# mLSTM cell and cosine-gated MLP on one core: the head's decay sums moved from VectorE subtractions to TensorE products and a GpSimd mask

## The chip, the cores and the metric

The kernel runs on 1 core of one Trainium2 chip. The metric is device time in microseconds of one execution; the figure compared is the median of several runs. A core has TensorE (PE in the profile; its weight loads are PEld), VectorE (DVE), ScalarE (ACT), GpSimd (POOL) and SyncE (SP), which here only issues DMAs.

## The reference

The program is an mLSTM cell with stabilised exponential gates, followed by an MLP whose gate is h cos h. Shapes: 4 batches, 8 heads, 768 steps, 40 dimensions a head; the MLP has 3072 rows, 320 to 2048 to 320.

```python
def _attn_ref(q, k, v, i_gate, f_gate, o_gate):
    for t in range(S):
        m_new = np.maximum(f_gate[:, :, t] + m, i_gate[:, :, t])
        f_stab = np.exp(f_gate[:, :, t] + m - m_new)
        i_stab = np.exp(i_gate[:, :, t] - m_new)
        m = m_new
        C = f_stab * C + i_stab * np.einsum('bhd,bhe->bhde', vt, kt)
        n = f_stab * n + i_stab * kt
        h_tilde = np.einsum('bhde,bhe->bhd', C, qt)
        denom = np.maximum(np.abs(np.einsum('bhd,bhd->bh', n, qt)), 1.0)
        y[:, :, t] = sigmoid(o_gate[:, :, t]) * h_tilde / denom

def _moe_ref(x, w_in, w_out):
    h = x @ w_in
    g = h * np.cos(h)
    return g @ w_out
```

## The kernel before, in words

The 768 steps are cut into six chunks of 128 (`NC`), and each chunk has four cells, one for each batch (`B`), with its eight heads: 24 cells, numbered n = 4 x chunk + batch. Inside a cell the recurrence is written as a masked matrix product. With F the running sum of f_gate, a = i_gate - F and M the running maximum of a, the weight of step s in the output of step t is exp(a[s] - M[t]) for s up to t and zero above. The tile `E` of a cell (128 source steps by 8 heads by 128 target steps) holds these weights; `decay` makes the exponential, `weigh` multiplies E by the scores k q (a product in PSUM), `values` multiplies by v, `normalize` divides by the denominator and applies the output gate into the tile y (one buffer), and `seam` turns y into the layout of the MLP and makes the cell's increment of the state from `kw` (`weigh_k`, on GpSimd). `seam_out` copies the turned y into xT and xL; `state` copies or adds the increment.

The order of all instructions is written by hand (`tc.manual_schedule()`): each engine runs its part of the list in that order, and waits in it hold up everything behind them on that engine. `first_cells` is the head: the four cells of chunk 0, the gates of all later chunks, and the first weights of the MLP. Then `first_period` starts the MLP of chunk 0 (`Up`: products L749 with w_in_sb, L743 with w_in_l; `near` on ScalarE, L757, is the first reader of their sums) along with cell 4, and the later functions pair MLP blocks with cells to the end.

In the head, the gates of chunk 0 are scanned first (`gates_first`). M and its exact split into three bfloat16 parts (`maxima_in_parts`) go to TensorE: for each cell `maxima_in` puts into two PSUM banks a wall of 1e30 above the diagonal (`wall_in`, L442) and on top the maxima spread over all source steps (`spread`, L449). `less_sums` (L467, VectorE) subtracts a from the banks into E, and `decay` takes exp(-E), so the wall becomes zero.

The gates of chunks 1 to 5 are in five tiles of 32 rows by 640: `gates_sums` (a scan on VectorE), `gates_less_sums` (GpSimd), `gates_maxima` (the second, long scan, and the write of M to DRAM, `M_d`), `gates_shifts`, `gates_carry` (five activations on ScalarE, and the write `G_d`), `gates_exp` (five activations on ScalarE: exp(a - the chunk's last maximum)), `gates_turn` (TensorE transposes of a and of that exponential, L325) and `gates_turn_out` (L328, one copy into `tab`, which the later cells read). `load_M` reads a cell's maxima back from M_d into E, spread over 128 rows (L436); `load_G_of` does the like with G_d.

The weights come as doubles and are turned into float32 in pieces: `take_apart` (ScalarE, L175 and L177), `bound` (VectorE, L181 and L182), `join` (VectorE, L191), `round_up` (GpSimd, L196). `weights_in(0)` issues the loads of three such pieces on SyncE: pieces 0 and 1 of w_in (L163, four DMAs each) and the piece w_in_l (L217). `warm` (L1096) issues products of zeros whose result nobody reads. PSUM is handed out in four rotating banks in the pool `ps_o`, two in `ps_a` and two in `ps_u`; a bank is given again when its last reader is done. `odd_constants` is four GpSimd memsets.

Of the kernel before, what the change touches and what calls it, by code (L numbers as in the profile page):

```python
# [11 lines left out]
FP = mybir.dt.float32  # L12
I32 = mybir.dt.int32
U32 = mybir.dt.uint32
BF = mybir.dt.bfloat16
AF = mybir.ActivationFunctionType
OP = mybir.AluOpType
# [12 lines left out]
def kernel(  # L30
# [56 lines left out]
    yo = small[:, 384:384 + DM]  # L87
    M0_parts = small[:, 704:768].bitcast(BF)
    of_parts = small[:, 768:784].bitcast(BF)
    nc.vector.memset(nil, 0.0)  # L90
    ident = const.tile([128, 128], FP, name="ident")
    make_identity(nc, ident)
# [6 lines left out]
    firsts = blocks[:, 32:36]  # L99
    nc.vector.memset(M0_parts, 0.0)  # L100
    nc.vector.memset(of_parts, 0.0)

    nc.gpsimd.memset(wall, 0.0)
    nc.gpsimd.affine_select(out=wall, in_=wall, compare_op=OP.is_ge, fill=1.0e30, base=0,
# [134 lines left out]
    m0 = gates.tile([BH, R], FP, name="m0")  # L239
    nM1 = gates.tile([BH, R], FP, name="nM1")  # L240
    dd = gates.tile([BH, R - 1, BH], FP, name="dd")

    def gates_constants():
        nc.gpsimd.memset(keep, 1.0)
# [22 lines left out]
    def maxima_in_parts():  # L267
# [7 lines left out]
        nc.vector.tensor_copy(out=M0_parts[2 * BH:3 * BH], in_=rest)  # L275
        nc.scalar.copy(out=M0_parts[BH:2 * BH], in_=mid)

    def gates_first_out():
        pg = ps_o.tile([128, 2, BH], FP, name="pg", tag="o")
        for j, src in enumerate((a0, e0)):  # L280
            nc.tensor.transpose(pg[:, j], src, ident[0:BH, 0:BH])
        nc.vector.tensor_copy(out=tab[:, 0, 0:2], in_=pg)
# [1 line left out]
    last = slice(C - 1, C)  # L284
    flat = [t.rearrange("r c s -> r (c s)") for t in (F1, M1, a1, keep, shift)]

    eW, eG = shift, keep

    def gates_sums():
        nc.vector.tensor_tensor_scan(out=flat[0], data0=flat[3], data1=flat[0], initial=0.0, op0=OP.mult, op1=OP.add)  # L290

    def gates_less_sums():
        nc.gpsimd.tensor_tensor(out=a1, in0=a1, in1=F1, op=OP.subtract)
        nc.gpsimd.tensor_copy(out=shift[:, 0, 0:1], in_=F0[:, last])
        nc.gpsimd.tensor_copy(out=shift[:, 1:R, 0:1], in_=F1[:, 0:R - 1, last])
# [15 lines left out]
        for j in range(2):  # L311
            nc.gpsimd.dma_start(out=dst[j], in_=eG[j:BH:2])

    def gates_exp():
        for c in range(R):
            nc.scalar.activation(out=eW[:, c], in_=a1[:, c], func=AF.Exp, bias=nM1[:, c:c + 1])

    def gates_diagonal():

        nc.vector.tensor_tensor(out=dd, in0=ident[0:BH, 0:BH].unsqueeze(1).to_broadcast([BH, R - 1, BH]),  # L320
                                in1=eG[:, 0:R - 1, last].to_broadcast([BH, R - 1, BH]), op=OP.mult)

    def gates_turn(pg, j):
        for c in range(R):
            nc.tensor.transpose(pg[:, c, j], (a1, eW)[j][:, c], ident[0:BH, 0:BH])  # L325

    def gates_turn_out(pg):
        nc.scalar.copy(out=tab[:, 1:NC, 0:2], in_=pg)  # L328

    def gates_spread():  # L330
        pd = ps_o.tile([128, R - 1, BH], FP, name="pd", tag="o")
# [38 lines left out]
    def sigmoid(c, bs=slice(0, B)):  # L370
        if c == 0:
            o = sig[c][:, bs]
            nc.scalar.activation(out=o, in_=o, func=AF.Sigmoid)
            return
        place_gates(c, AF.Sigmoid)
# [92 lines left out]

    def decay(n, heads=range(H)):
        c, b = divmod(n, B)  # L470
        if n < B:
            nc.scalar.activation(out=Es[n], in_=Es[n], func=AF.Exp, scale=-1.0)
            return
        for h in heads:
            g = b * H + h
            nc.scalar.activation(out=Es[n][:, h], in_=Es[n][:, h], func=AF.Exp, scale=-1.0, bias=tab[:, c, 0, g:g + 1])  # L476
# [91 lines left out]
    def values(n):  # L568
        pool, tag = psum(n)
        E = Es[n]  # L570
        if n < B:
            ph = pool.tile([128, H, D1], FP, name="ph", tag=tag)
            for j in range(2):
                for p in range(HP):
                    h = 2 * p + j
                    nc.tensor.matmul(ph[:, h], E[:, h], vs(n)[:, h, 0:D1], start=True, stop=True)  # L576
            heads_of[n] = ph
            return
        vt = pool.tile([128, 4, C], FP, name="vt", tag=tag)
        state = st[n % B]  # L580

        for i in range(3):
            if i < 2:
                for a in range(HP):
                    h = 2 * a + i
                    nc.tensor.matmul(vt[32 * a:32 * a + 32, i], vs(n)[:, h, 0:32], E[:, h], start=True, stop=False)  # L586
            else:
                for a in range(HP):
                    nc.tensor.matmul(vt[32 * a:32 * a + 32, i], vr2[n // 2 % 2][:, n % 2, a, 1:3].rearrange("q g d o -> q (g d o)"),
                                     E[:, 2 * a + 1], start=True, stop=False)  # L590
                for a in range(HP):
                    nc.tensor.matmul(vt[32 * a:32 * a + 16, i], vr2[n // 2 % 2][:, n % 2, a, 0].rearrange("q d o -> q (d o)"),
                                     E[:, 2 * a], start=False, stop=False)
            for a in range(HP):
                nc.tensor.matmul(vt[32 * a:32 * a + 32, i], state[:, ts(HP * i + a, 32)], Gs[n][:, a], start=False, stop=True)  # L595
        heads_of[n] = vt
# [501 lines left out]
    def maxima_in(n):  # L1098
        for i in range(2):
            wall_in(n, i, psum_o())  # L1100
        for i in range(2):
            spread(n, i)

    def less_sums(n):
        for i in range(2):
            decay_exponents_half(n, i)

    def first_cells():
        gates_in()
        nc.scalar.copy(out=ident_b, in_=ident)  # L1110
        for i in range(3):
            r = ts(i, BH)
            nc.scalar.copy(out=of_parts[r], in_=ident[r, r])
        load(0, "qk")
        gates_constants()
        ones_of_values()
        later_gates_in()
        load(0, "v")
        load(1, "qk")
        load_o(0)  # L1120
        load(1, "v")
        load(2, "qk")
        warm(9)
        wall_in(0, 0, pmu)
        gates_first()
        for n in range(B):
            load_E(n)
        load(2, "v")
        load(3, "qkv")
        maxima_in_parts()  # L1130
        gates_first_out()
        wall_in(0, 1, psum_o())
        for i in range(2):
            spread(0, i)
        for i in range(2):
            decay_exponents_half(0, i)
        turn(0)
        turn_out(0, False)
        decay(0)
        maxima_in(1)  # L1140
        less_sums(1)
        weigh_k(0)
        blocks_constants()
        weigh_k(1)
        state_constants()
        scores(0)
        turn(1)
        decay(1)
        turn_out(1, False)
        weigh(0)  # L1150
        sigmoid_next()
        sigmoid(0)
        exp_next()
        gates_sums()
        gates_less_sums()
        values(0)
        pieces.extend(weights_in(0))
        scores(1)
        weigh(1)
        maxima_in(2)  # L1160
        less_sums(2)
        decay(2)
        values(1)
        normalize(0)
        normalize(1)
        maxima_in(3)
        less_sums(3)
        turn(2)
        turn_out(2, False)
        weigh_k(2)  # L1170
        seam(0)
        seam_out(0)
        scores(2)
        state(0)
        decay(3)
        weigh(2)
        seam(1)
        seam_out(1)
        weigh_k(3)
        gates_maxima()  # L1180
        gates_shifts()
        load_M(B)
        load_blocks(B)
        load(B, "kv")
        outs.append((0, weights_out(0)))
        turn(3)
        turn_out(3, False)
        values(2)
        normalize(2)
        state(1)  # L1190
        gates_carry()
        load_G_of(B)
        load_blocks(B + 1)
        pg = ps_a.tile([128, R, 2, BH], FP, name="pg", tag="a")
        gates_turn(pg, 0)
        scores(3)
        take_apart(*pieces[0])
        seam(2)
        weigh(3)
        bound(pieces[0][0])  # L1200
        seam_out(2)
        gates_exp()
        take_apart(*pieces[1])
        warm(2, psum_o())
        values(3)
        join(*pieces[0])
        round_up(*pieces.pop(0))
        state(2)
        more = weights_in(1)
        pieces.append(next(more))  # L1210
        normalize(3)
        warm(6, psum_o())
        gates_turn(pg, 1)
        bound(pieces[0][0])
        put_together(*pieces.pop(0))
        pieces.append(next(more))
        decay_exponents(B)
        seam(3)
        seam_out(3)
        gates_turn_out(pg)  # L1220
        take_apart(*pieces[0])
        bound(pieces[0][0])
        put_together(*pieces.pop(0))
        gates_diagonal()
        pieces.extend(more)
        outs.append((1, weights_out(1)))
        load_M(B + 1)
        load_G_of(B + 1)
        load(B + 1, "kv")
        outs.append((2, weights_out(2)))  # L1230
        low_dimensions(B)
        turn_blocks(B)
        state(B - 1)
        decay(B)
        odd_constants()
        odd_values_of(B)
        weigh_k(B)
        scale_q(B)
# [4 lines left out]
    def sigmoid_next():  # L1243
        nc.scalar.activation(out=spot[:, 1:2], in_=spot[:, 0:1], func=AF.Sigmoid)
# [410 lines left out]
```

## Time and profile before

| | before |
|---|---|
| median of 3 runs | 506.22 us (503.96 to 506.45) |
| profiled execution, own time | 503.72 us |
| its span | 501.9 us |
| busy in the span: PE, DVE, ACT, POOL | 99%, 84%, 66%, 60% |
| granted TensorE clock | 1.00 |
| first MLP product (L749) starts | 31.89 us |
| first `near` (L757) starts | 37.29 us |

The span is the profiled program from its first to its last instruction; the execution's own time is 1.8 us more. Lines of the chain of waits give start, length and what; lines of a timeline give start, busy time, engine, line, operation, the tiles written and read, their shapes and a count, and in brackets the idle time just before with what ended it.

### The profile page before, as it was taken

How to read it: one execution, taken by the hardware profiler on the slowest of the kernel's cores; microseconds unless marked ns; L12 is line 12 of the kernel's file. 1: busy time of each engine (PE TensorE's matmuls, PEld its weight loads, DVE VectorE, ACT ScalarE, POOL GpSimd, SP SyncE). 2: the span in 40 equal slices, each digit the busy share in tenths (PEclk: the TensorE clock that was granted, in tenths of full speed). 3: DMA queues.
4: the chain of work that ended last, by engine and by line, in shares of the span. 5: the costliest groups of instructions: out<-in, count | busy, mean ns of one | idle time of the engine just before them, and what ended most of it. 6: DMA issues, size and time to landing. Idle time of an engine off the chain costs nothing.

```text
span 501.9 us, 11143 instructions
## 1 busy us (share of the span) xinstructions
PE 495.1 (99%) x4038; PEld 375.4 (75%) x4038; DVE 420.6 (84%) x842; ACT 332.5 (66%) x646; POOL 300.0 (60%) x394
## 2 busy tenths in 40 slices
PE   9999999999999999999999999999999999999997
PEld 6856656565667668887887888788788888787876
DVE  7899998999878878899889889889979866777565
ACT  6799997878564575765877846777847743443541
POOL 8254557666555576787558877657567446434340
PEclk9999999999999999999999999999999999999999
DMA  9989899997366346129446118628113000010001
GB/s 139 182 223 239 213 224 279 233 217 136 114 178 111 101 120 127 50 86 202 132 125 106 48 54 195 168 83 150 43 35 85 1 7 5 2 54 0 2 0 54
DMA packets 100663, 56.74 MB, mean 113 GB/s; under 512 B 63456, under 2 KB 93360, under 8 KB 100608
## 3 DMA queue, kind: packets, MB, share of 16 engines
q1 hardware_dynamic: 97408, 54.43, 46.8%
q10 hardware_dynamic: 2896, 1.23, 1.0%
q8 instruction: 32, 0.52, 0.5%
q0 software_dynamic: 304, 0.36, 0.3%
q14 instruction: 23, 0.19, 0.1%
HBM read 50.66 MB, written 4.10 MB: 109 GB/s over the span
## 4 chain that ended last, share of the span: by engine, by line
PE 85%; ACT 4%; DVE 3%; DMA 2%; SPq 2%; POOL 2%; issue 1%; DVEq 0%; ACTq 0%; POOLq 0%
PE acc L1014 24%; PE pup L817 17%; PE pup L749 9%; PE po L863 6%; PE pup L833 6%; PE late L1014 5%; PE ps L560 4%; PE pup L743 3%; PE vt L595 2%; PE vt L586 2%; PE pu L701 2%; PE ph L576 1%; DMA E<-M_d 1%; DMA vs<-in_v_dram 1%; DVE n L760 1%
## 5 line engine op out<-in xcount | busy, mean ns | idle before, releaser
L757 ACT ACTIVATE n<-pup 128x512 int32<-128x512 f32 x64 | 37.0, 593 | 84.2 <-DVE pup L842 58.4
L765 ACT ACTIVATE n<-n 128x512 f32<-128x512 f32 x96 | 57.7, 626 | 16.5 <-DVE n L760 12.5
L852 POOL TENSOR_TENSOR g<-g,n 128x512 f32<-128x512 f32 x31 | 39.6, 1278 | 47.5 <-ACT n L765 47.4
L749 PE MATMUL pup<-xT,w_in_sb 128*128 128x512 f32 x128 | 58.7, 601 | 0.3 <-ACT xT L712 0.2
L1014 PE MATMUL acc<-w_out_sb,g 128*128 128x160 f32 x320 | 58.7, 303 | 0.0
L760 DVE SCALAR_TENSOR_TENSOR n<-pup,n 128x512 f32<-128x512 f32 x64 | 43.1, 689 | 18.5 <-ACT n L757 15.9
L834 POOL TENSOR_TENSOR blocks<-blocks 128x256 f32<-128x256 f32 x32 | 25.1, 785 | 54.5 <-ACT blocks L826 54.5
L1014 PE MATMUL acc<-T,g 128*128 128x160 f32 x304 | 56.4, 301 | 0.0
L817 PE MATMUL pup<-xT,w_in_sb 128*128 128x256 f32 x192 | 53.5, 385 | 0.2
L476 ACT ACTIVATE E<-E,tab 128x128 f32<-128x128 f32 x160 | 50.1, 389 | 4.3 <-POOL E L462 4.1
L1014 PEld LDWEIGHTS acc<-w_out_sb,g 128*128 128x128 f32 x320 | 49.0, 190 | 4.7 <-issue 2.7
L769 DVE TENSOR_TENSOR g<-pup,n 128x512 f32<-128x512 f32 x64 | 42.7, 687 | 5.7 <-ACT n L765 4.8
L1014 PEld LDWEIGHTS acc<-T,g 128*128 128x128 f32 x304 | 46.5, 190 | 1.1 <-issue 0.4
L749 PEld LDWEIGHTS pup<-xT,w_in_sb 128*128 128x128 f32 x128 | 23.1, 189 | 30.7 <-issue 30.0
L825 ACT COPY blocks<-pup 128x512 f32<-128x512 f32 x32 | 18.6, 582 | 34.2 <-PE pup L817 33.8
L817 PEld LDWEIGHTS pup<-xT,w_in_sb 128*128 128x128 f32 x192 | 33.8, 189 | 9.6 <-ACT blocks L826 4.4
L817 PE MATMUL pup<-x_room,room 128*128 128x256 f32 x128 | 38.5, 382 | 0.0
L542 POOL TENSOR_TENSOR qG<-t,G 128x512 f32<-128x512 f32 x20 | 26.4, 1321 | 16.7 <-DVE t L538 16.7
L1014 PE MATMUL acc<-T,blocks 128*128 128x160 f32 x160 | 36.2, 308 | 0.2 <-POOL blocks L904 0.2
L863 PE MATMUL po<-w_out_sb,g 128*128 128x320 f32 x128 | 36.2, 436 | 0.1
L833 PE MATMUL pup<-xL,w_in_l 64*128 64x512 f32 x128 | 36.1, 641 | 0.0
L566 DVE TENSOR_TENSOR E<-ps,E 128x512 f32<-128x512 f32 x46 | 29.5, 682 | 5.8 <-PE ps L560 5.6
(227 smaller groups left out, 1210.7 us busy)
## 6 DMA issues: line engine op xcount, KB each, us to landing
E<-M_d SPq DMA_DIRECT2D x20, 512.0 KB, 6.0
qr<-in_q_dram SPq DMA_DIRECT2D x72, 80.0 KB, 2.6
kr<-in_k_dram SPq DMA_DIRECT2D x72, 80.0 KB, 2.2
bits<-in_moe_w_out_dram SPq DMA_DIRECT2D x8, 640.0 KB, 6.2
G<-G_d SPq DMA_DIRECT2D x18, 256.0 KB, 5.7
blocks<-in_moe_w_in_dram SPq DMA_DIRECT2D x32, 128.0 KB, 4.6
out_dram<-o_sb SPq DMA_DIRECT2D x23, 160.0 KB, 1.8
o<-in_o_gate_dram SPq DMA_DIRECT2D x40, 80.0 KB, 4.4
```

The costliest lines, as they stand in the source:

```text
L476: nc.scalar.activation(out=Es[n][:, h], in_=Es[n][:, h], func=AF.Exp, scale=-1.0, bias=tab[:, c, 0, g:g + 1])
L566: nc.vector.tensor_tensor(out=w, in0=pss[n][j], in1=w, op=OP.mult)
L749: nc.tensor.matmul(pu.rearrange("p (b t) -> p b t", b=B), w_in_sb[:, i, ts(2 * f2 + e, 128)], xT[c][:, i:NK * B:NK], start=(i == 0 and not ...
L757: nc.scalar.activation(out=self.n[e], in_=self.pu[e], func=AF.Copy, bias=0.25)
L760: nc.vector.scalar_tensor_tensor(out=self.n[e].bitcast(FP), in0=self.pu[e], scalar=0.25, in1=self.n[e], op0=OP.add, op1=OP.subtract)
L765: nc.scalar.activation(out=r, in_=r, func=AF.Sin, scale=TWO_PI_DOWN)
L769: nc.vector.tensor_tensor(out=g, in0=self.pu[e], in1=self.n[e].bitcast(FP), op=OP.mult)
L817: nc.tensor.matmul(bank[:, part].rearrange("p (b t) -> p b t", b=B // 2), w[:, f2], x, start=start, stop=stop, skip_group_check=True)
L833: nc.tensor.matmul(pu, w_in_l[r, f2], xL[c][r].rearrange("p b t -> p (b t)"), start=False, stop=True, skip_group_check=True)
L852: tt(out=self.g, in0=self.g, in1=self.n[e].bitcast(FP), op=OP.mult)
L863: nc.tensor.matmul(po[c][b], gs[c, f][:, ts(b, C)], w_out_sb[:, f], start=(f == 0), stop=(f == NF - 1))
L1014: nc.tensor.matmul(a, lhs, rhs, start=start, stop=stop)
```

## The change

For cells 2 and 3 the wall and the subtraction go. `sums_in_parts` makes three bfloat16 parts of -a (on VectorE, with one copy on ScalarE), as `maxima_in_parts` does of M. `exponents_in` lets TensorE put -a into the bank by a product with these parts, and `spread` adds M. `decay` reads the two banks itself, one activation for each, and GpSimd then sets what lies above the diagonal to zero in E (`affine_select`). Cells 0 and 1 keep the old way.

`gates_exp` goes. `gates_last` makes a diagonal tile `dM` of the negative last maxima (VectorE), `gates_less_last` adds in PSUM the turned a and the last maximum by ten products, and `gates_turn_out` takes the exponential on the way into `tab`.

The order in `first_cells` is written anew from cell 0's sigmoid on: `gates_maxima` right after cell 3's products, `odd_constants` in the head, `load_blocks(B)` and `load(B, "kv")` ahead of `load_M(B)`, `take_apart`, `bound` and `join` of the first piece earlier, `normalize(2)` later, and the two calls of `warm` in the head's second half left out.

```diff
+    a0_parts = small[:, 784:848].bitcast(BF)
+    nc.vector.memset(a0_parts, 0.0)
+    dM = gates.tile([BH, R, BH], FP, name="dM")
...
+    def sums_in_parts():
+        rest, mid = blocks[0:BH, 38], blocks[0:BH, 39].bitcast(BF)[:, 0:C]
+        hi = a0_parts[0:BH]
+        nc.vector.tensor_scalar(out=hi, in0=a0, scalar1=-1.0, scalar2=None, op0=OP.mult)
+        nc.vector.scalar_tensor_tensor(out=rest, in0=a0, scalar=-1.0, in1=hi, op0=OP.mult, op1=OP.subtract)
+        nc.vector.tensor_copy(out=mid, in_=rest)
+        nc.vector.tensor_tensor(out=rest, in0=rest, in1=mid, op=OP.subtract)
+        nc.vector.tensor_copy(out=a0_parts[2 * BH:3 * BH], in_=rest)
+        nc.scalar.copy(out=a0_parts[BH:2 * BH], in_=mid)
+
+    def exponents_in(n):
+        for i in range(2):
+            m = pm[n, i] = psum_o()
+            g = n * H + HP * i
+            nc.tensor.matmul(m, a0_parts, of_parts[:, g:g + HP].unsqueeze(2).to_broadcast([128, HP, C]),
+                             start=True, stop=False)
+            spread(n, i)
...
-    def gates_exp():
-        for c in range(R):
-            nc.scalar.activation(out=eW[:, c], in_=a1[:, c], func=AF.Exp, bias=nM1[:, c:c + 1])
+    def gates_last():
+        nc.vector.tensor_tensor(out=dM, in0=ident[0:BH, 0:BH].unsqueeze(1).to_broadcast([BH, R, BH]),
+                                in1=nM1.unsqueeze(2).to_broadcast([BH, R, BH]), op=OP.mult)
...
+    def gates_less_last(pw):
+        for c in range(R):
+            nc.tensor.matmul(pw[:, c], a1[:, c], ident[0:BH, 0:BH], start=(c == 0), stop=False)
+            nc.tensor.matmul(pw[:, c], one.to_broadcast([BH, 128]), dM[:, c], start=False, stop=(c == R - 1))
+
+    def gates_turn_out(pg, pw):
+        nc.scalar.copy(out=tab[:, 1:NC, 0], in_=pg)
+        nc.scalar.activation(out=tab[:, 1:NC, 1], in_=pw, func=AF.Exp)
...
     def decay(n, heads=range(H)):
+        if n < 2:
+            nc.scalar.activation(out=Es[n], in_=Es[n], func=AF.Exp, scale=-1.0)
+            return
         if n < B:
-            nc.scalar.activation(out=Es[n], in_=Es[n], func=AF.Exp, scale=-1.0)
+            E = Es[n]
+            for i in range(2):
+                nc.scalar.activation(out=E[:, ts(i, HP)], in_=pm[n, i], func=AF.Exp, scale=-1.0)
+            nc.gpsimd.affine_select(out=E, in_=E, compare_op=OP.is_ge, fill=0.0, base=0,
+                                    pattern=[[0, H], [1, C]], channel_multiplier=-1)
             return
...
         sigmoid_next()
+        sums_in_parts()
+        gates_sums()
         sigmoid(0)
         exp_next()
-        gates_sums()
         gates_less_sums()
+        odd_constants()
         values(0)
         pieces.extend(weights_in(0))
         scores(1)
         weigh(1)
-        maxima_in(2)
-        less_sums(2)
+        exponents_in(2)
         decay(2)
         values(1)
         normalize(0)
         normalize(1)
-        maxima_in(3)
-        less_sums(3)
+        exponents_in(3)
+        gates_maxima()
+        gates_shifts()
         turn(2)
         turn_out(2, False)
         weigh_k(2)
+        decay(3)
         seam(0)
+        load_blocks(B)
+        load(B, "kv")
+        load_M(B)
+        outs.append((0, weights_out(0)))
+        scores(2)
         seam_out(0)
-        scores(2)
+        weigh(2)
+        turn(3)
+        turn_out(3, False)
+        take_apart(*pieces[0])
         state(0)
-        decay(3)
-        weigh(2)
         seam(1)
         seam_out(1)
         weigh_k(3)
-        gates_maxima()
-        gates_shifts()
-        load_M(B)
-        load_blocks(B)
-        load(B, "kv")
-        outs.append((0, weights_out(0)))
-        turn(3)
-        turn_out(3, False)
-        values(2)
-        normalize(2)
-        state(1)
         gates_carry()
         load_G_of(B)
         load_blocks(B + 1)
-        pg = ps_a.tile([128, R, 2, BH], FP, name="pg", tag="a")
-        gates_turn(pg, 0)
+        pgs = ps_a.tile([128, 2, R, BH], FP, name="pg", tag="a")
+        gates_turn(pgs[:, 0])
         scores(3)
-        take_apart(*pieces[0])
-        seam(2)
+        bound(pieces[0][0])
+        state(1)
+        values(2)
         weigh(3)
-        bound(pieces[0][0])
-        seam_out(2)
-        gates_exp()
-        take_apart(*pieces[1])
-        warm(2, psum_o())
-        values(3)
         join(*pieces[0])
         round_up(*pieces.pop(0))
-        state(2)
+        take_apart(*pieces[0])
+        gates_last()
+        normalize(2)
+        values(3)
         more = weights_in(1)
         pieces.append(next(more))
+        seam(2)
+        seam_out(2)
+        state(2)
         normalize(3)
-        warm(6, psum_o())
-        gates_turn(pg, 1)
         bound(pieces[0][0])
         put_together(*pieces.pop(0))
         pieces.append(next(more))
         decay_exponents(B)
+        gates_less_last(pgs[:, 1])
         seam(3)
         seam_out(3)
-        gates_turn_out(pg)
+        gates_turn_out(pgs[:, 0], pgs[:, 1])
...
         decay(B)
-        odd_constants()
         odd_values_of(B)
```

More of the change, by code (lines that the diff above doesn't have):

```diff
@@ L285 @@
     flat = [t.rearrange("r c s -> r (c s)") for t in (F1, M1, a1, keep, shift)]
-    eW, eG = shift, keep
+    eG = keep
     def gates_sums():
@@ L321, in gates_diagonal, with gates_turn @@
                                 in1=eG[:, 0:R - 1, last].to_broadcast([BH, R - 1, BH]), op=OP.mult)
-    def gates_turn(pg, j):
+    def gates_turn(pg):
         for c in range(R):
-            nc.tensor.transpose(pg[:, c, j], (a1, eW)[j][:, c], ident[0:BH, 0:BH])
-    def gates_turn_out(pg):
-        nc.scalar.copy(out=tab[:, 1:NC, 0:2], in_=pg)
+            nc.tensor.transpose(pg[:, c], a1[:, c], ident[0:BH, 0:BH])
+    def gates_less_last(pw):
[5 more added lines that the diff above has]
+        nc.scalar.activation(out=tab[:, 1:NC, 1], in_=pw, func=AF.Exp)
     def gates_spread():
```

## The prediction

> **What bounds it now.** I read the page first, then the chain of waits up to 66 us, then each engine's timeline and the DMA queue up to 60 us. The page's busy table and, after it, pieces of the chain of waits (start, length, what):
>
> ```profile
> PE 495.1 (99%) x4038; PEld 375.4 (75%) x4038; DVE 420.6 (84%) x842; ACT 332.5 (66%) x646; POOL 300.0 (60%) x394
> ```
>
> ```profile
> 10.04 4.20 DMA vs<-in_v_dram
> ...
> 14.38 1.95 PE ph L576 x16
> ...
> 26.58 0.54 PE pm L1096 x2
> 27.11 1.71 PE ph L576 x16
> 28.82 1.30 PE pm L1096 x6
> ...
> 31.37 0.03 ACT xT L712
> ...
> 34.82 0.94 ACT E L476 x3
> ```
>
> TensorE is full to the end, so the head counts only by when it hands over. From the landing of cell 1's v (14.24) to the first product of the second block (31.89) TensorE works without a hole, but 8 of its matmuls are `warm` fillers (L1096, 6 in 1.47 us: 0.22 each). Behind that, ScalarE's queue (tables, low dimensions, state, decay of cell 4) sets when `near` starts, at 37.29, just after the products end. From there TensorE, VectorE and ScalarE are all packed, so a shift of `near` goes 1:1 into the end. TensorE's timeline at the handover, and VectorE's beside it:
>
> ```profile
> 28.65 1.47 PE L1096 MATMUL pm<-room 128*128 128x512 bf16 x6
> 30.05 0.49 PE L325 MATMUL pg<-ident,w_out_sb 32*128 32x32 f32 x5
> 30.54 0.41 PE L692 MATMUL px<-ident,y 128*128 128x128 f32 x2
> ...
> 31.89 3.67 PE L749 MATMUL pup<-xT,w_in_sb 128*128 128x512 f32 x8 [0.23 <-ACT xT L712]
> 36.11 1.13 PE L743 MATMUL pup<-xL,w_in_l 64*128 64x512 f32 x4 [0.56 <-POOL w_in_l L196]
> ...
> 38.53 0.48 PE L332 MATMUL pd<-dd,one 32*128 32x128 f32 x2
> ```
>
> ```profile
> 31.98 0.28 DVE L714 COPY xL<-px 128x128 f32<-128x128 f32 x1
> 32.44 1.19 DVE L181 TENSOR_SCALAR w_in_l<-w_in_l 128x256 f32<-128x256 f32 x1 [0.18 <-ACT w_in_l L175]
> 33.66 1.06 DVE L182 TENSOR_SCALAR w_in_l<-w_in_l 128x256 int32<-128x256 int32 x1
> ```
>
> SyncE's queue, where w_in's first pieces (L163) and the first E (L436) are issued:
>
> ```profile
> 17.59 4.42 SPq L163 DMA_DIRECT2D blocks<-in_moe_w_in_dram  x8
> 22.37 2.71 SPq L217 DMA_DIRECT2D blocks<-in_moe_w_in_dram  x4
> 26.70 0.36 SPq L436 DMA_DIRECT2D E<-M_d  x1
> ```
>
> The four issues of piece 0 are the first half of those 4.42 us, the fourth at 19.72. The same line lands 4.0 to 4.8 us after issue (the tile's DMA view), so piece 0 is whole at about 23.7. E waits 1.6 us for M_d.
>
> **Up to the long scan: nothing.** The added memset (0.11, as L100) lies before f_gate's landing, where VectorE waits 0.54. `sums_in_parts` costs VectorE five small operations, as `maxima_in_parts` (3.71 to 5.26: 1.55 us), between weigh(0) and the first scan: 10.10 to 11.65, scan (1.68) to 13.3. weigh(1) started at 13.31 anyway, for its scores; if that cover were gone the 1.55 us would show in full. Its ScalarE copy (0.30) falls into the 0.77 us in which ScalarE waits for og. `gates_less_sums` on GpSimd moves behind the scan, to 13.4 to 15.2, then `odd_constants` (four memsets, 1.25 us) to 16.5; GpSimd idled 5.5 us there.
>
> **Cells 2 and 3.** The wall matmuls (L442) become products of the same shape, 0.22 each: even. Four subtractions (L467, 1.28 a pair) leave VectorE: -2.56. Each decay's one activation (1.05) becomes two from PSUM (as L757, 0.59): even. Two masks (L462, 1.12 each) come to GpSimd. A new wait: decay must empty cell 2's first bank before cell 3's second product. ScalarE has its table at 16.05, so that product runs at 16.7, and all behind it on TensorE (turn(2), seam(0), scores(2)) is late by 0.1.
>
> GpSimd masks cell 2 at 17.2 to 18.35. normalize(0) follows weigh(1) at once (14.5), normalize(1) at 16.36; its y waits until seam(0) has read the one y buffer, 18.82 (18.72 before). The scan follows at 19.3 (21.59 before), M_d is issued at 21.2; behind that DMA on GpSimd stand m0, weigh_k(2) and the mask of cell 3 (23.05 to 24.2). weigh(2) is done at 22.6 (21.67 before).
>
> **The new wait.** VectorE's next instruction is now `bound` of w_in's piece 0, which stood after weigh(3). It needs ScalarE's take_apart (0.66), and that the landing at 23.7: bound starts at 24.45, after 1.9 us idle. Queued behind it on VectorE: weigh(3), join, `gates_last`, both normalizes; behind take_apart on ScalarE: state(0), seam_out(1), gates_carry. So: bound to 25.45, weigh(3) to 26.7, join (0.69) to 27.3, dM (32x160, as L320 0.27) to 27.6, normalize(2) (1.55) to 29.15. The 2.56 us taken off VectorE come back as this wait and the later place of normalize(2). TensorE does values(3) at 26.1 to 27.9, waits, and seam(2) (1.02) runs 29.2 to 30.22; y(3) is done at 30.75 (30.53 before).
>
> One rule bears on bound: the Trainium skill, "SBUF — State Buffer", Who interferes with whom, says that VectorE's tensor_scalar in its two-port mode and a GpSimd operation exclude each other for the whole instruction. The two rows above agree: L181 and L182 (0.56 and 0.29 at 52 us) took 1.19 and 1.06, ending 0.15 after round_up (33.48) and 0.14 after the mask of cell 4 (34.58). By it bound would wait for weigh_k(3) until 24.9, and the sum would be 0.1 higher.
>
> **The tables.** `gates_exp` goes: five activations, -1.47 us of ScalarE, but these lie ahead of take_apart(1), which waits for nothing late. `gates_turn_out` becomes a copy and an exponential of 160 columns: about +0.1 against L328. On TensorE 5 transposes become 10 true f32 matmuls (`gates_less_last`) between seam(2) and seam(3). Such a form does not stand in the trace. Lower bound, the transposes (L325: 5 in 0.49, 0.07 apart): 10 x 0.07 = 0.7. Upper: L332, one f32 matmul of the same weights, two records, 0.22 from first to next weights' end (L576, 41 columns, has its records 0.107 apart): 10 x 0.215 = 2.15. I take 2.15, since true f32 matmuls have two records in every row of the trace. They end at 32.37, and seam(3) begins there instead of at 30.54: +1.83. From there the queue is as before: xT +0.83 (33.20), first product +0.52 (33.72); ScalarE tables, take_apart of w_in_l, low dimensions, state(3), decay of cell 4, and near at 39.2 instead of 37.29: **+1.9 us**. With 0.7 it is +0.45.
>
> **Moved queues.** SyncE has the blocks of cell 4 and its k, v (6 issues) ahead of E: they fill the 1.6 us wait, and E is issued at 28.0 instead of 26.70. Landing 4.5 to 6.7 us later (6.7: the second E) it is there by 34.7, its mask done by 35.9, and decay of cell 4 is not due before 36.7: hidden by 0.8 us. gates_carry is 1.1 us later (27.6), so G_d lands at 32.4 and SyncE loads G at about 32.4, as now. The memsets off GpSimd at 36.0 to 37.25 free nothing: values of cell 4 wait for weigh, not for qG (39.39).
>
> **Sum.** The profiled execution took 503.72 (span 501.9, 1.8 around it); the sum makes it 505.6. It is 2.5 below the median of the runs (506.22), one of which is as low (503.96); the shift added to the median gives 508.1.
>
> **Rivals.**
> 1. *Faster*: the lighter queues win. TensorE's work from 14.38 without the 1.76 us of fillers, and with the transposes' price, would let the first product start 1.7 us earlier: 504.5. For it: VectorE loses 1.1 us of work net, and the scan moves up 2.3 us. Against: piece 0 would have to land before 22.6. Decides: whether bound starts at weigh(2)'s end. 0.13.
> 2. *Slower, the clock*: fillers are gone and TensorE now idles 0.7 us (25.4) and 1.3 us (27.9) inside 4 us. The first rows show the price of a cold array: L1096 0.43 apart until 4.2 us, 0.22 after. If it falls back there, gates_less_last and seam(3) take twice their 3.2 us: +1.9 +3.2, 511.3. Against: after the one 0.56 us hole (35.56) products stay 0.43 apart as before it. Decides: a hole long enough. 0.12. The Trainium skill, "TensorE: Matmul & The Clock Gate", What's actually happening, lets the clock fall after an idle window of about 3.4 us; by that rule no hole here is long enough, and the longest in the trace tests nothing.
> 3. *Slower, a late load*: E lands over 7.6 us after issue, or G_d's rows come late behind E, k and v: each us beyond the 0.8 of cover adds one; at 2 us, 510. 0.13.
>
> **Numbers.** The forecast has 0.62. This kernel's measurement tells about 0.5% (2.5 us) from no change. The forecast spreads from +0.4 to +2.7 (matmul price, landing by 0.5) around a median that itself moves by over 1 us: mostly within. Slower by over 0.5%: rivals 2 and 3 and a tenth of all from the forecast's upper end, 0.33; faster needs more than rival 1 can give, 0.07; within 0.60. Range: from rival 1 (504.5) to halfway between rivals 3 and 2 (510.5).
>
> **What would show it.** Right: VectorE idle for over 1.5 us before `bound` in the head, released by ScalarE's take_apart; 20 records in `gates_less_last` about 0.11 apart; seam(3) near 32.4, first product near 33.7, near at 39.2. Wrong: the first product before 32; less_last under 1 us; matmuls 0.43 apart where 0.22 is due; decay of cell 4 waiting for GpSimd's mask.

## The result, and the profile after

Over four runs each the kernel after takes 511.75 us (511.39 to 511.95) and the kernel before 505.14 (503.96 to 506.45): ratio 1.0129, 95% interval 1.0096 to 1.0163, about 6.5 us slower. The profiled execution took 511.39 us with a span of 509.7, 7.8 more than before, at a mean granted clock (the share of its full clock that TensorE was given) of 0.986. In 85 later runs of the kernel before, the 13 with a mean clock of 0.997 took 506.3 to 507.3 us and 69 of the other 72 took 503.2 to 505.3, so the 505.14, with two of its four runs at 506, lies high.

The clock row of the profile's page, in tenths of full speed, shows where: before it is 9 in all 40 slices, after it sinks in slices 2 to 4 (13 to 51 us).

```profile
PEclk9878999999999999999999999999999999999999
```

TensorE's timeline at the handover (columns as before). Cell 1's values wait 0.96 us; seam(2) waits 1.01 us more; then everything is stretched: ten products of 0.43 us each in `gates_less_last` (L352, L353), the seam in 1.88 where 1.02 is due, and the first MLP product at 39.65 instead of 31.89.

```profile
15.49 1.98 PE L612 MATMUL ph<-vs,E 128*128 128x41 f32 x16 [0.96 <-DVE E L602]
...
31.48 0.69 PE L728 MATMUL px<-ident,y 128*128 128x128 f32 x2 [1.01 <-DVE y L694]
...
33.36 0.63 PE L352 MATMUL pg<-ident,w_out_sb 32*128 32x32 f32 x2
33.81 0.61 PE L353 MATMUL pg<-dM,one 32*128 32x32 f32 x2
...
37.77 0.69 PE L728 MATMUL px<-ident,y 128*128 128x128 f32 x2
...
39.65 4.67 PE L785 MATMUL pup<-xT,w_in_sb 128*128 128x512 f32 x8
```

The windows of the trace for 35 to 40 us: length, busy time and count of PE, PEld, DVE, ACT and POOL, granted clock, DMA share, GB/s. TensorE is busy all the time at half clock, VectorE works 0.29 us of 5 (4.38 before): all wait for the slow products.

```profile
35.00:40.00 5.00, 5.00 (x37) 4.49 (x37) 0.29 (x1) 0.88 (x4) 2.32 (x2) 0.50 0.90 231
```

ScalarE's first `near`, at 37.29 before, now waits for the products, though its own queue had moved late with the seam:

```profile
45.41 1.09 ACT L793 ACTIVATE n<-pup 128x512 int32<-128x512 f32 x2 [0.33 <-PE pup L779]
```

VectorE's timeline, and then GpSimd's, show who made the holes. L285, the first operation of `sums_in_parts` (32 x 128), took 2.04 us and ended 0.08 after GpSimd's state memsets (L136); `bound` (L183 and L184; L181 and L182 before, 0.50 and 0.51) took 2.57 beside the mask of cell 3 (L507) and `weigh_k` (L517).

```profile
10.18 2.04 DVE L285 TENSOR_SCALAR room<-blocks 32x128 bf16<-32x128 f32 x1
...
25.21 1.75 DVE L183 TENSOR_SCALAR w_in_sb<-w_in_sb 128x512 f32<-128x512 f32 x1 [0.32 <-ACT w_in_sb L177]
27.00 0.82 DVE L184 TENSOR_SCALAR w_in_sb<-w_in_sb 128x512 int32<-128x512 int32 x1
```

```profile
10.65 1.49 POOL L136 MEMSET st<- 128x384 f32 x4
...
25.59 1.08 POOL L507 TENSOR_SCALAR_AFFINE_SELECT blocks<-blocks 128x1024 f32<-128x1024 f32 x1
26.65 0.88 POOL L517 TENSOR_TENSOR kw<-room,tab 128x320 f32<-128x320 f32 x1
```

The granted clock changes only at multiples of 3.41 us from its first rise: after, it is 0.5 in 17.74 to 21.15 (one stretch) and in 31.39 to 41.63 (three), else 1.00.

### The profile page after: what moved, and what is told of

Same layout as the page of the kernel before. It is cut to its first block, busy times and chain, and to the rows that moved or that the text cites. A ratio compares the mean times of both kernels' runs of the same rounds, so it can differ in the third digit from the quotient of the medians.

```text
span 509.7 us, 11160 instructions
## 1 busy us (share of the span) xinstructions
PE 501.3 (98%) x4045; PEld 381.9 (75%) x4045; DVE 420.7 (83%) x845; ACT 331.7 (65%) x645; POOL 302.7 (59%) x396
## 3 DMA queue, kind: packets, MB, share of 16 engines
q10 hardware_dynamic: 2896, 1.23, 1.0%
## 4 chain that ended last, share of the span: by engine, by line
PE 86%; DVE 5%; ACT 4%; SPq 2%; issue 1%; POOL 1%; DMA 1%; DVEq 0%; ACTq 0%
PE acc L1050 25%; PE pup L853 18%; PE pup L785 10%; PE pup L869 6%; PE po L899 6%; PE late L1050 4%; PE ps L596 4%; PE pup L779 3%; PE vt L631 2%; PE vt L622 2%; PE pu L737 2%; DVE n L796 1%; DMA og<-in_o_gate_dram 1%; PE vt L625 1%; PE vt L628 1%
## 5 line engine op out<-in xcount | busy, mean ns | idle before, releaser
L853 PE MATMUL pup<-x_room,room 128*128 128x256 f32 x128 | 38.5, 382 | 0.0
L878 DVE TENSOR_TENSOR pup<-pup,blocks 128x256 f32<-128x256 f32 x32 | 13.9, 435 | 24.4 <-PE pup L869 24.0
```

The source lines that it names most:

```text
L853: nc.tensor.matmul(bank[:, part].rearrange("p (b t) -> p b t", b=B // 2), w[:, f2], x, start=start, stop=stop, skip_group_check=True)
```

## The experiments

Three theories were weighed. **Clock**: the holes and the thin products (little of the array at work) let the clock fall, and the half clock makes the loss. **Tables**: the ten products themselves, on the path between seam(2) and seam(3), cost it. **Order**: the waits on VectorE and GpSimd in the new order cost it, whatever the clock. All ratios below are to the kernel before, run on the same chip, with 95% intervals; "near" is the start of the first `near` in the profiled run (37.29 before, 45.41 after).

**e1_fill.** The kernel after, with fillers again, where TensorE had its holes.

```diff
+        warm(5)
         values(1)
...
+        warm(6, psum_o())
         seam(2)
```

> The changed kernel with fillers put back: warm(5) ahead of values(1), warm(6) ahead of seam(2), nothing else moved. Theory 1 (the time goes to the granted TensorE clock, which fell to half at 17.74 to 21.15 and 31.39 to 41.63 us because TensorE had holes of 1.0 us in the windows before): the clock stays at 1.00 in both stretches, gates_less_last takes 2.1 instead of 4.4 us, the first MLP product starts at about 34 instead of 39.7, near at about 40 instead of 45.4, and the time is 5 to 6 us below the changed kernel's. Rival (the holes come from VectorE's queue and the clock costs little because VectorE ends last anyway): under 1.5 us gained, near after 44.

509.65 us, ratio 1.0096 (1.0066 to 1.0125), near at 43.36. No fall at 17.7 any more, and `gates_less_last` began at full clock (0.22 a product). But in its midst, at 33.46, the clock fell for two stretches, and normalize(2)'s y product took 1.84 us beside GpSimd. The gain is 2.1 us by the medians, not the 5 to 6 expected: the fillers ahead are not enough, the ten products themselves do not hold the clock.

**e2_memsets.** The kernel after, with `state_constants` behind `odd_constants`, so that no memset stands beside `sums_in_parts`.

```diff
         weigh_k(1)
-        state_constants()
...
         odd_constants()
+        state_constants()
```

> The changed kernel with the four state memsets of GpSimd moved behind odd_constants, out of the time of sums_in_parts. Theory 2 (the root is that the first operation of sums_in_parts, tensor_scalar 32x128, was held for 2.04 us by these memsets, which made weigh(1) 1.5 us late and the first hole on TensorE): that operation takes about 0.4 us, weigh(1) starts at about 13.4, the hole of 0.96 us ahead of values(1) is gone, the clock does not fall at 17.7 us, seam(0) comes 2.3 us earlier, and the time falls by 2 to 4 us if the second fall of the clock (31.4 us) goes with it, by about 2 if not. Rival: the first hole is absorbed by the landing of v or by bound, and the time stays within 1 us of the changed kernel.

511.15 us, ratio 1.0123 (1.0093 to 1.0153), near at 44.31. The first hole went, and the fall at 17.7 with it; L285 took 0.20 us. But normalize(2)'s y product then met GpSimd's G_d issue (28.73 to 29.84) and `round_up` (29.86 to 31.15) and took 2.18 where 0.56 to 0.68 is due, in VectorE's timeline of this kernel:

```profile
10.92 0.20 DVE L285 TENSOR_SCALAR room<-blocks 32x128 bf16<-32x128 f32 x1
...
29.06 2.18 DVE L694 TENSOR_TENSOR y<-room,dn 128x256 f32<-128x256 f32 x2
```

The clock was 0.5 from 30.0 to 40.23. The memsets' place is worth 0.3 us of the 6.5 by the two ratios and 1.1 by the profiled spans (509.7 and 508.6), less than the 2 to 4 expected and close to what these can tell apart.

**e3_both.** Both edits.

> Both edits: fillers back and the state memsets moved. If the clock and the held operation are the whole of the loss, the time comes to that of the forecast's sum, 1.9 us above the kernel before (gates_less_last still between seam(2) and seam(3), bound still waiting for piece 0): about 507. If fillers alone do all of it, it equals the run with fillers alone within 0.7 us.

508.69 us, ratio 1.0076 (1.0045 to 1.0107), but the profiled run (510.72) still had the clock at 0.5 in 27.91 to 34.74 and again in 38.15 to 41.57, near at 44.72. The fillers and the memsets together take off 2.7 us by the ratios; over half of the loss stays, and the 507 expected is missed.

**e4_nofill.** The kernel before, without the fillers that the change leaves out.

```diff
-        warm(2, psum_o())
         values(3)
...
-        warm(6, psum_o())
```

> The kernel before without the two calls of warm in the head's second half (2 and 6 fillers), nothing else changed. Theory 1 (a hole of about 1.4 us in one window of 3.4 us is enough to halve the clock): the clock falls to 0.5 around 31.5 us for at least one window of 3.4 us, the first products run 0.85 us apart, and the time rises by 1.7 to 4 us. Rival (only an idle window halves it, and the changed kernel's clock fell for another reason): the clock stays at 1.00 and the time is within 0.7 us of the kernel before.

505.59 us, ratio 1.0017 (0.9997 to 1.0038), near at 40.10. In the profiled run the clock fell for one stretch (33.0 to 36.41), and v of cell 1 landed late (16.41, 14.24 before). All ten runs have a mean clock of 0.993 to 0.997: the clock falls, as expected, but the old order stands it for 0.9 us by the ratio instead of 1.7 to 4. Alone it is no cause of 6.5 us.

**e5_products.** The kernel before with the products and masks of cells 2 and 3 alone; the memsets moved as in e2.

```diff
         sigmoid_next()
+        sums_in_parts()
...
-        maxima_in(2)
-        less_sums(2)
+        exponents_in(2)
...
-        maxima_in(3)
-        less_sums(3)
+        exponents_in(3)
```

> The kernel before in its own order with the products and masks alone (parts of -a made where sigmoid's table loads, exponents_in and the GpSimd mask for cells 2 and 3), gates_exp, the tables and both calls of warm as before; the state memsets stand behind gates_less_sums, so that they don't hold the first operation. Theory (the order and the tables lose, not the products): TensorE's queue is still full up to the first MLP product, that starts at 31.5 to 32.5 us, the clock stays at 1.00, and the time is within 0.8 us of the kernel before. Rival (the masks on GpSimd come late to weigh): weigh(2) or weigh(3) waits for GpSimd, the first product is over 1.5 us later and the time 1.5 us or more above.

504.99 us, ratio 1.0014 (0.9998 to 1.0029), clock 1.00, near at 37.76. The 2.56 us taken off VectorE buy nothing: weigh(2) still waits for its scores, the long scan starts as before (21.62), and the carry waits 1.44 us for GpSimd (1.01 before), which now has the masks and whose weigh_k(3) took 1.89 us beside the long scan, 0.72 in e11_scan, where the scan lies elsewhere.

**e6_tables.** The kernel before with the new tables alone, in its own order and with its fillers.

```diff
-        gates_exp()
         take_apart(*pieces[1])
+        gates_last()
...
         warm(6, psum_o())
-        gates_turn(pg, 1)
+        gates_less_last(pg[:, 1])
```

> The kernel before with the tables alone: gates_exp replaced by gates_last, the ten f32 products of gates_less_last in place of the second five transposes, and the exponential in gates_turn_out; all else, fillers included, as before. Theory 1: the ten products take 2.1 us at full clock ahead of seam(3), 1.7 more than the transposes, and hardly count as activity (32 rows, 32 columns of the array's 128 by 512), so the clock falls for a window or two after them; the first MLP product starts at 33.6 or later and the time is 1.7 us above the kernel before if the clock holds, 3 to 5 if it falls. Rival (the products fit under normalize(3)): within 0.7 us.

506.72 us, ratio 1.0044 (1.0026 to 1.0062), near at 40.70: 2.2 us by the ratio, 3.2 by the profiled spans (3 to 5 expected if the clock fell). TensorE's timeline has no hole but the 0.22 us ahead of the first MLP product, which the kernel before has too; the ten products take 0.22 each at full clock (30.56 to 32.91), and yet the clock falls behind them, from 34.22 to 37.63: the first products take 5.34 us instead of 3.67.

```profile
32.59 0.38 PE L326 MATMUL pg<-dM,one 32*128 32x32 f32 x2
32.91 0.44 PE L703 MATMUL px<-ident,y 128*128 128x128 f32 x2
...
34.28 5.34 PE L760 MATMUL pup<-xT,w_in_sb 128*128 128x512 f32 x8 [0.22 <-ACT xT L723]
```

**e7_exp.** e2_memsets with the tables undone: `gates_exp` and five transposes instead of `gates_last` and ten products; still no fillers.

```diff
-        gates_last()
+        gates_exp()
...
-            nc.tensor.matmul(pw[:, c], a1[:, c], ident[0:BH, 0:BH], start=(c == 0), stop=False)
-            nc.tensor.matmul(pw[:, c], one.to_broadcast([BH, 128]), dM[:, c], start=False, stop=(c == R - 1))
+            nc.tensor.transpose(pw[:, c], shift[:, c], ident[0:BH, 0:BH])
```

> The changed kernel with the state memsets moved (as in the second run) and the tables undone: gates_exp on ScalarE and five transposes in place of gates_last and gates_less_last, no fillers. Theory 1: less low-activity work, so the cold stretch is one window (3.4 us) and not three, near comes 3 to 4 us earlier than with the memsets moved alone (44.3), and the time is 2.5 to 4 us below that run's, near 507.5 to 508.5. Rival (the cold clock comes from the missing fillers alone and lasts as long without the small products): within 1 us of that run.

506.88 us, ratio 1.0054 (1.0035 to 1.0073), near at 41.12; clock 0.5 in 27.44 to 37.68, three stretches. From e2 to e7 the ratio loses 0.0069, 3.5 us: as much as the ten products cost at half clock (10 x 0.43 less the transposes' 0.74). The time came as expected, but not for the reason given: the clock stays down for three stretches, as in e2, and not for one.

**e8_fill_exp.** e7 with fillers in the three holes.

```diff
+        warm(5)
         values(1)
...
+        warm(3, psum_o())
         values(3)
...
+        warm(6, psum_o())
         seam(2)
```

> The same with fillers: warm(5) ahead of values(1), warm(3) ahead of values(3), warm(6) ahead of seam(2). If clock, held operation and small products are the whole loss, the clock stays at 1.00 through the head and what is left is the order: VectorE waits for piece 0, normalize(2) comes late, first MLP product at 32.5 to 33, the time 0.5 to 1.5 us above the kernel before. If over 2 us are left, there is a further cause in the order.

505.9 us, ratio 1.0029 (1.0011 to 1.0046), clock 1.00 to the end, near at 39.00. The first MLP product starts at 33.53 (32.5 to 33 expected). About 1.5 us stay (0.6 to 2.3 by the interval): the order's own price. VectorE's timeline and GpSimd's of this kernel name a wait of that size, normalize(2)'s y product again (2.03, 1.35 over its 0.68):

```profile
28.68 2.03 DVE L697 TENSOR_TENSOR y<-room,dn 128x256 f32<-128x256 f32 x2
```

```profile
28.18 1.12 POOL L335 DMA_DIRECT2D G_d<-w_out_sb  x2 [2.48 <-ACT w_out_sb L332]
29.31 1.31 POOL L198 TENSOR_TENSOR w_in_sb<-w_in_sb,blocks 128x512 int32<-128x512 int32 x1
```

That this wait is the whole 1.5 us was not tried by itself.

**e9_spread.** e6 with its six fillers put among the ten products.

```diff
+            warm(2 if c == 0 else 1, bank)
             nc.tensor.matmul(pw[:, c], a1[:, c], ident[0:BH, 0:BH], start=(c == 0), stop=False)
```

> The kernel before with the tables of the change alone, as e6_tables, but the six filler products stand between the ten products of gates_less_last (two, then one ahead of each further pair) instead of ahead of them; same work, same count. Theory 1: narrow products (32 rows, 32 columns) hardly count for the clock, and in e6_tables they alone, without any hole, brought it down in 34.22 to 37.63. With the fillers among them each 3.41 us stretch holds enough full-width work: granted clock 1.00 throughout, the first near at 39.3 to 39.7 instead of 40.70, span 503.7 to 504.2, ratio 1.002 to 1.0035. Rival: the fall comes from something else in that stretch (the kind of product, a wait that the records do not show): the clock falls again, near at 40.7, span about 505, ratio 1.0044.

A miss: 508.49 us, ratio 1.0085 (1.0059 to 1.011), the clock at 0.5 for two stretches (32.93 to 39.76) instead of one, near at 42.31. The fillers among float32 products stand 0.32 from start to start of the next, so one group (a filler, two products) takes 0.87 us for a filler's 0.22 of full work: the stretch from 29.52 was thinner than in the count behind the expectation. The rival's reading, that the fall has another cause, is told apart by the next experiment.

**e13_narrow.** The kernel before, its last eight fillers on 32 rows of the array instead of 128.

```diff
-            nc.tensor.matmul(bank or pw, nil, nil.unsqueeze(1).to_broadcast([128, HP, 128]), start=True, stop=True)
+            nc.tensor.matmul(bank, nil[0:32], nil[0:32].unsqueeze(1).to_broadcast([32, HP, 128]), start=True, stop=True)
```

> The kernel before, its last eight fillers (two ahead of values(3), six behind it) made with 32 of the 128 rows instead of all 128: the same count, the same 512 columns streamed and the same 0.22 us each, a quarter of the array. It asks what the clock counts. Theory 1 (the share of the array that works, over stretches of 3.41 us; so far it fell at 0.35 and below and held at 0.37 and above): the stretch with the six fillers goes from 0.61 to about 0.32, so the clock falls for at least one stretch near 31 to 38 although TensorE has no hole there, near at 38.5 to 40.5, time 0.5 to 1.5 us above the kernel before, ratio 1.001 to 1.004. If the stretches lie so that the sum is 0.4, it holds and tells nothing. Rival (the share of time in which columns stream, 0.82 in that stretch, whatever the rows): clock 1.00 from 5 us on, near at 37.3, ratio 1.000.

505.54 us, ratio 1.0014 (0.9993 to 1.0034), near at 38.12. TensorE's timeline is the old one up to the handover, with no hole and the same 1.46 us of fillers; the clock was 0.5 from 31.40 to 34.81. `near` came a little earlier than the 38.5 to 40.5 expected. Of the ten runs seven have a mean clock of 0.993 to 0.997, against 13 of the 85 of the kernel before. Three have 0.999 or 1.00; the expectation had allowed for stretches that lie otherwise (the first rise of the clock comes at 4.02 to 6.96 us in the fourteen profiles).

```profile
28.89 1.46 PE L1100 MATMUL pm<-room 32*128 32x512 bf16 x6
30.20 0.44 PE L325 MATMUL pg<-ident,w_out_sb 32*128 32x32 f32 x5
...
31.94 5.09 PE L749 MATMUL pup<-xT,w_in_sb 128*128 128x512 f32 x8
```

The stretch with these fillers and the one behind it, in the columns of the windows above: TensorE is busy for all of the first, and the clock is down in the second.

```profile
27.99:31.40 3.41, 3.41 (x36) 2.45 (x37) 2.87 (x10) 3.19 (x11) 1.29 (x1) 1.00 1.06 271
31.40:34.81 3.41, 3.35 (x20) 1.66 (x15) 3.14 (x5) 3.25 (x12) 2.39 (x2) 0.50 0.97 250
```

So neither a hole nor idle columns are needed. What counts is how much of the array works. I counted it for all fourteen profiled kernels: for each matmul record the time of its columns at 512 in 0.216 us (five fillers in e1_fill, 14.51 to 15.59), a float32 record twice that (those of the first MLP product before start 0.43 apart), times the share of rows and columns that its weights fill, summed over each 3.41 us stretch of the head. At full clock:

| what followed | filled share of the stretch |
|---|---|
| fell | 0.15 (e4), 0.16 (after), 0.21 (e1, e12), 0.22 (e2, e3, e6, e7), 0.28 (e9), 0.29 (after, at 14.33), 0.33 (e13), 0.35 (e3) |
| held | 0.37 (e2), 0.42 (e1), 0.43 (after, e8, e11) and all above |

The time in which columns stream does not separate them: e13's stretch with 0.78 fell, e3's with 0.44 held. At half clock a column takes twice the time; counted so, the clock rose after 0.73 and more and stayed down after 0.62 and less. As work that is 0.37 and 0.31, so one limit, between 0.35 and 0.37 of what a stretch holds at full clock, sorts the rises with the falls. The limit is fitted to these kernels, and it hangs on the double weight of float32: counted once, stretches that fell reach 0.27 and stretches that held go down to 0.18. That width counts does not hang on it: e13 changes nothing but the rows of the fillers.

**e11_scan.** An attempt at a better version: e5 with the long scan ahead of normalize(1), and four fillers fewer.

```diff
         normalize(0)
+        gates_maxima()
         normalize(1)
...
         turn_out(2, False)
+        gates_shifts()
...
-        warm(2, psum_o())
         values(3)
...
-        warm(6, psum_o())
+        warm(4, psum_o())
...
         seam(3)
+        take_apart(*pieces[0])
         seam_out(3)
         gates_turn_out(pg)
-        take_apart(*pieces[0])
```

> e5_products (the kernel before with the products and masks alone) with the long scan ahead of normalize(1) and its shifts ahead of weigh_k(2), take_apart of w_in_l ahead of seam_out(3), and four fillers fewer (warm(2) gone, warm(6) to warm(4)). Theory: the head's second half hangs on scan, shifts, carry on ScalarE; ScalarE waited 1.44 us for GpSimd's m0 ahead of the carry. With the scan 3 to 4 us earlier that wait goes, near moves from 37.76 to 36.4 to 36.9, and the time is 0.9 to 1.4 us below e5_products: ratio 0.998 to 0.9995. The fillers left keep the clock at 1.00. Rival: another wait takes its place (seam(1) behind a later normalize(1), E or the mask of cell 4): near about 37.5, ratio 1.001; or the thinner filling lets the clock fall: ratio 1.003 or more.

503.63 us, ratio 0.9984 (0.9967 to 1.0001), clock 1.00, near at 37.11. The scan ran at 16.18 instead of 21.62, and the carry's wait is gone, but `near` misses the 36.4 to 36.9 expected, since a new wait took half of the gain, on ScalarE: the decay of cell 4 waits for its mask, which stands behind `round_up` on GpSimd.

```profile
34.63 2.45 ACT L505 ACTIVATE E<-E,tab 128x128 f32<-128x128 f32 x8 [0.61 <-POOL E L484]
```

It is the lowest of all, by less than the interval can tell from the kernel before.

**e12_scan_before.** The same moves in the kernel before, with its subtractions.

> The kernel before with the same moves as e11_scan, but its own subtractions and no products. Theory: the scan's place is worth the same here: near 0.8 to 1.2 us ahead of 37.29, ratio 0.997 to 0.999; the products are not needed for it. Rival: the subtractions of cells 2 and 3 stand in the way (scan not before 17.9, weigh(2) later), or the clock falls: ratio 1.000 or more, and e11_scan is the better of the two.

504.3 us, ratio 0.9999 (0.9982 to 1.0016). No gain, against the 0.997 to 0.999 expected; in its profiled run (near at 40.03) TensorE waited 1.41 us for v of cell 1, which put the clock down once (17.81 to 21.22), so that profile says little on the scan's place.

## Why the prediction was wrong

The forecast was +1.9 us with the first product at 33.72; it came at 39.65. The 5.93 us between them are, step by step from the timeline: seam(2) starts at 31.48 instead of 29.2 (+2.28), it takes 1.88 up to `gates_less_last` instead of 1.02 (+0.86), the ten products take 4.41 up to seam(3) instead of 2.15 (+2.26), and from there to the first product 1.88 instead of 1.35 (+0.53). The last three are the half clock, 3.65 us; of the first, 1.5 us is `bound` held beside GpSimd, and the rest its later start. A sign that the prediction itself had named for being wrong came, products 0.43 apart where 0.22 is due; its sign for being right, VectorE idle for over 1.5 us before `bound`, did not (0.32).

- **The step that failed most: rival 2's deciding point**, "a hole long enough". The mechanism was named, but it got 0.12, because the holes were judged as too short, and the sum was worked out at full clock. That its time of 511.3 is close to the 511.75 measured is luck: it starts from the median of 506.22, 2.5 us above the profiled execution. From the profiled execution the same sum gives 503.72 + 1.9 + 3.2 = 508.8, against 511.39, and the 2.28 us at seam(2) is not in it. In the stretch from 27.98 to 31.39 TensorE had a hole of 0.29 us and most of the one of 1.01, and its other work there was narrow (`values`, 41 columns): 0.16 of the array. e13_narrow shows that no hole is needed at all. The argument against it (products that stayed slow after a 0.56 us hole) tested nothing, as the full-width products around that hole fill 0.54 of the stretch (and those behind it start in pairs, 0.53 apart, not 0.43). The Trainium skill, "TensorE: Matmul & The Clock Gate", What's actually happening, has the clock in two states and set by free-running windows of about 3.41 us, and the traces agree (0.5 and 1.00, changes 3.41 us apart); its condition for the fall, an idle window, they contradict if idle means without work.
- **The fillers** were priced as spare time only ("TensorE's work from 14.38 without the 1.76 us of fillers"). Six of them are 6 x 0.216 = 1.3 us of full work, 0.38 of a stretch; made a quarter as wide (e13) they left 0.33 of the 0.61. Leaving them out alone costs the old order 0.9 us by its ratio, which the interval does not tell from nothing (e4); with narrow products and holes in the same stretches the clock stays down for three of them.
- **"Up to the long scan: nothing"** failed in its term: `sums_in_parts` took 3.2 us (10.18 to 13.37) instead of 1.55, because the state memsets ran beside it; weigh(1) started at 14.78 instead of 13.31. The row it was sized by, `maxima_in_parts`, ran beside GpSimd memsets too, and yet its first operation, a cast of the same shape, took 0.36 before and 0.26 after; why L285 was held so much longer is open. From there the first fall follows at 17.74, and from that a late seam(0), y of cell 1 at 21.48 (3.01 us idle) and the scan at 21.95 instead of 19.3. Taken away (e2: scan at 19.70) it changes the end by only 0.3 us by the ratios and 1.1 by the spans, since the next conflict takes its place.
- **"One rule bears on bound"** named the right conflict and undersized it: +0.1 was said; L183 and L184 took 2.57 instead of 1.01, and take_apart on ScalarE, behind the late copies of turn(3), let them start at 25.21 instead of 24.45. Together that is the 2.28 us at seam(2). The mask of cell 3 was to be over by 24.2; behind the late scan it ran at 25.59, on top of `bound`. Where the scan is early (e2, e8), `bound` takes 0.86 to 1.26 and the same kind of wait falls on normalize(2)'s y product, 2.03 to 2.18.
- **`gates_less_last`**: the form was right. True float32 products cost 0.22 each, the upper price, in e6 and at the start in e1; at half clock they cost 0.43.
- **Right**: the products of cells 2 and 3 are even on TensorE and the lighter VectorE buys nothing (e5); piece 0 is read on landing at 23.9 in e8 (23.7 said); late loads cost nothing, decay of cell 4 (42.62) waited for no mask; a faster kernel (rival 1) did not come. That a shift of `near` goes nearly 1:1 into the end holds too: +8.12 and +7.8 in the span here, +3.41 and +3.2 in e6, +0.83 and +0.9 in e13.

With the ratios in a row: order with fillers +1.5 us (e8), without fillers +2.7 (e7), with the ten products +6.2 (e2), with the memsets in their place +6.5 (7.4 against the 504.34 that e2 was compared with). The parts done alone in the old order (e4, e5, e6) add up to 3.8 by their ratios. The rest is most likely that thin products, missing fillers and late VectorE work fall into the same stretches and keep the clock down over four of them; no run has the whole change at a clock of 1.00, so how the rest splits is not shown.

## What to carry to other kernels

Before taking filler products out, or putting narrow products (few rows, few columns) into a stretch that leads into full-width work, add up how much of the array each 3.4 us will fill; here a third was too little, even without a hole. And work that is moved from VectorE to GpSimd is not off VectorE: read which VectorE operations will run beside it, and allow each that is held up to the neighbour's whole length.

## What the hardware showed beyond expectation

- The clock fell after stretches of up to 0.35 filled share and held from 0.37. Once down, it rose after the same 0.37 of work, which at half clock fills 0.73 of a stretch, and stayed down at 0.31 (0.62 of the time, e9).
- A 32 x 128 tensor_scalar from float32 to bfloat16 took 2.04 us beside GpSimd memsets, 1.23 in e1, 0.20 without, though a cast of the same shape took only 0.26 to 0.36 beside other memsets; normalize(2)'s y product, a tensor_tensor with both inputs in SBUF, took 1.47 to 2.19 beside GpSimd's G_d issue and `round_up` (e1, e2, e3, e7, e8), and normalize(3)'s 0.56 in the same kernels. The Trainium skill, "SBUF — State Buffer", Who interferes with whom, states both locks; the traces agree but for that cast, and give their sizes here.
- Changing between products on 128 rows and on 32 rows cost TensorE about 0.1 us each time: 0.32 from a filler's start to the next product in e9, against 0.22 in a row of one kind. It is not the change from bfloat16 to float32: from the last 128-row filler to the float32 `values` on 128 rows it took 0.22 (before, 26.74 to 26.95), from the last 32-row filler to the 32-row transposes 0.22 (e13, 29.99 to 30.20), but from a 32-row filler to the 128-row `values` 0.30 (e13, 26.68 to 26.98).
